# Cosine attention and a low-rank mixer with an MLP: a rebuild on 128-row token chunks, with the MLP cut into pieces placed by hand

## The chip, the cores and the metric

The kernel runs on one core of one Trainium2 chip. The metric is the device time of one execution in microseconds (us), the median of several. A core has TensorE (PE: matmuls, with its weight loads shown apart as PEld), VectorE (DVE), ScalarE (ACT), GpSimd (POOL) and SyncE (SP). PE writes its results into PSUM, which has eight banks; DVE and ACT carry them from there to SBUF. DMAs bring data from HBM to SBUF and back; here POOL and SP issue them. Each engine runs its own instructions in a fixed order and waits on semaphores for the others.

## The reference, cut to what matters

```python
# batch, heads, seq, head_dim = 8, 12, 448, 64;  rank 32;  d_model 768
q_n = q / (norm(q) + 1e-6);  k_n = k / (norm(k) + 1e-6)
scores = q_n @ k_n.T / tau                    # tau = 0.1
attn = exp(scores - max(scores));  attn /= sum(attn) + 1e-9
x = (attn @ v), heads side by side            # [8, 448, 768]
h = x.T @ U @ V                               # mixes the 448 tokens through rank 32
u = x + h.T
out = u + relu(u @ w_ch1) @ w_ch2             # 768 -> 3072 -> 768
```

Inputs and output are float32 in HBM. Both kernels compute in bfloat16 and accumulate in float32. Both leave the maximum out of the softmax, since a cosine over tau stays between -10 and 10.

## The kernel before, in words

The 448 tokens of a batch are held as 4 chunks of 112 rows (`SC = 4`, `SCH = 112`; token `4*s + c` is row s of chunk c). Heads go in pairs, 6 pairs a batch, 48 pairs in all.

`attention_pair` (L91 on) issues six DMAs from POOL's queue, which turn float32 into bfloat16 on the way (q L101, k L105, v L109). DVE squares and sums q and k (L118 to L121); ACT takes the logarithm (L124) and two exponentials (L125, L127), which give 1/norm; DVE scales q (L131). PE transposes q and k, 112 columns at a time (L138, L143). The two heads of a pair then lie in rows 0 to 63 and 64 to 127. DVE copies the transposed q out (L149) and writes the transposed k twice, once with the lower and once with the upper 64 rows zeroed by a mask (L151, L153), so that a score matmul over all 128 rows gives one head. There are 8 score matmuls a pair, 112 rows by 448 (L160), each followed by an exponential on ACT (L166), which carries 1/norm of k as its scale. The product with v is 32 matmuls a pair, 65 columns wide (L178); column 65 of v is one, so it gives the sum of the softmax. DVE divides (L185, L187) into `X_sb`.

`moe_stage0` transposes X (L199, L204), multiplies with U (L210, L216) and V (L221), and DVE adds h to the transposed X (L227). `moe_mlp1` (L235, L241) makes 24 chunks of 128 hidden units: 6 matmuls of 448 columns and one ReLU on ACT each. `moe_mlp2` (L248, L254) has the second weight matrix as the loaded operand and gives the transposed output, 6 chunks of 24 matmuls of 448 columns. `moe_store` transposes it back (L264, L270) and stores it from SP's queue (L271).

The MLP of a batch is emitted in 7 pieces between the pairs of the next batch (`emit_moe_piece`); a scheduler then orders each engine's instructions. The weights come in 30 DMAs from POOL's queue among the loads of batch 0 (L89). PSUM: two banks each for scores, av, transposes and everything of the mixer and the MLP.

## Time and profile before

| what | value |
|---|---|
| time, 3 runs | 819.03, 822.45 and 1068.92 us; median 822.45 |
| profiled execution: first to last instruction | 818.3 us |
| PE busy in it | 715.8 us (87%) |
| ACT busy | 494.6 us (60%), with 94 table loads in it |
| DVE busy | 307.0 us (38%) |
| POOL busy | 225.8 us (28%) |
| first MLP matmul of batch 0; of batch 7 | at 106.5 us; at 753.6 us |
| granted PE clock, mean | 0.991 |

The profiled execution lies 0.7 us under the fastest run and 4.1 us under the median, so what lies around the span is small; one of the three runs stands far off the two others. A row of the timeline gives start, length, engine, line, operation, written tile `<-` read tiles, shape, the number of instructions merged into it, and in brackets the idle time before it with what ended it. A row of the groups gives `busy us, mean ns of one`. Matmuls overlap in their pipeline, so the length of one is longer than its share of a stream: the rate is read from a merged row. In this program the stages are: batch 0's attention alone (to 106 us), seven stretches with the attention of one batch and the MLP of the one before, and the last MLP alone (from 753.6 us).

### The profile page before, as it was taken

The numbers are of one execution on the slowest core, as the hardware profiler recorded it, in microseconds if no ns is written. First come the engines' busy times: TensorE is split into PE (matmuls) and PEld (weight loads), VectorE is DVE, ScalarE is ACT, GpSimd is POOL, SyncE is SP. The second block draws the span as 40 slices with busy tenths as digits, with TensorE's granted clock in tenths as the row PEclk, the third lists the DMA queues.
The fourth block names the chain that finished last, engine by engine and source line by source line (L and its number), as shares of the span: only waits on it lengthen the run. The fifth ranks groups of instructions, "written<-read, shape, count | busy, mean of one in ns | idle before, by whom it ended". The sixth has DMA issues, their size and how long they took to land.

```text
span 818.3 us, 12706 instructions
## 1 busy us (share of the span) xinstructions
PE 715.8 (87%) x5104; PEld 426.3 (52%) x5104; DVE 307.0 (38%) x720; ACT 494.6 (60%) x862; POOL 225.8 (28%) x382
## 2 busy tenths in 40 slices
PE   2456777999989998899989998899989999999996
PEld 2244544555555555555545555455545556554553
DVE  2253673444434362344524362334523351223000
ACT  3457688954786379755777369755778357622411
POOL 6388832422423232322423231322232100000000
PEclk9999999999999999999999999999999999999999
DMA  8999942524434261524434261433442120002002
GB/s 122 181 149 149 79 29 18 36 18 85 31 22 30 18 96 12 35 19 85 28 24 29 18 97 12 27 25 75 34 29 18 12 68 1 2 1 68 1 0 68
DMA packets 142618, 37.84 MB, mean 46 GB/s; under 512 B 135104, under 2 KB 138208, under 8 KB 142560
## 3 DMA queue, kind: packets, MB, share of 16 engines
q0 software_dynamic: 138464, 26.03, 38.6%
q1 hardware_dynamic: 4096, 11.01, 4.2%
q8 instruction: 40, 0.66, 0.3%
q14 instruction: 18, 0.15, 0.1%
HBM read 52.02 MB, written 11.01 MB: 77 GB/s over the span
## 4 chain that ended last, share of the span: by engine, by line
PE 61%; ACT 16%; issue 8%; DMA 8%; POOL 4%; DVE 2%; DVEq 0%; POOLq 0%; ACTq 0%
PE m_ps L248 26%; PE m_ps L235 15%; PE sc_ps L160 8%; PE av_ps L178 6%; ACT L124 4%; ACT L166 3%; ACT attn_uT L166 3%; DMA v_pair<-in_v_dram 3%; DMA w_sb<-in_moe_w_ch_dram 3%; ACT relu L241 2%; DMA q_pair<-in_q_dram 2%; PE o_ps L264 1%; PE h_ps L221 1%; POOL v_pair L109 1%; ACT O_sb L270 1%
## 5 line engine op out<-in xcount | busy, mean ns | idle before, releaser
L166 ACT ACTIVATE attn_uT<-sc_ps,inv_qk 112x448 bf16<-112x448 f32 x384 | 221.1, 633 | 102.3 <-PE sc_ps L160 99.0
L235 PE MATMUL m_ps<-uT_all,w_sb 128*128 128x448 bf16 x1152 | 250.2, 356 | 10.3 <-ACT relu L241 9.7
L248 PE MATMUL m_ps<-relu,w_sb 128*128 128x448 bf16 x1152 | 234.6, 352 | 0.0
L160 PE MATMUL sc_ps<-qT,kTz 128*112 128x448 bf16 x384 | 141.0, 389 | 41.8 <-ACT attn_uT L166 25.0
L178 PEld LDWEIGHTS <-attn_uT 112*112 112x112 bf16 x1536 | 124.5, 141 | 81.2 <-issue 33.2
L235 PEld LDWEIGHTS <-w_sb 128*128 128x128 bf16 x1152 | 106.8, 99 | 105.8 <-issue 23.2
L248 PEld LDWEIGHTS <-w_sb 128*128 128x128 bf16 x1152 | 107.7, 98 | 91.6
L241 ACT ACTIVATE relu<-m_ps 128x448 bf16<-128x448 f32 x192 | 101.0, 539 | 89.2 <-PE m_ps L235 89.0
L178 PE MATMUL av_ps<-v_pair,attn_uT 112*112 112x65 bf16 x1536 | 145.2, 221 | 3.2 <-ACT attn_uT L166 3.2
L109 POOL DMA_DIRECT2D v_pair<-in_v_dram x96 | 66.9, 701 | 271.9 <-issue 263.0
L105 POOL DMA_DIRECT2D k_pair<-in_k_dram x96 | 66.8, 701 | 98.5 <-PE qkT_ps L143 84.0
L270 ACT CAST O_sb<-o_ps 112x768 f32<-112x768 bf16 x32 | 23.2, 808 | 100.4 <-PE o_ps L264 100.4
L254 DVE TENSOR_TENSOR uT_all<-m_ps,uT_all 128x448 bf16<-128x448 f32 x48 | 29.9, 622 | 120.2 <-PE m_ps L248 120.2
L160 PEld LDWEIGHTS <-kTz 128*112 128x112 bf16 x384 | 52.2, 142 | 42.3 <-DVE kTz L151 24.9
L101 POOL DMA_DIRECT2D q_pair<-in_q_dram x96 | 67.1, 704 | 9.1 <-DVE qn_pair L131 3.6
L118 DVE TENSOR_TENSOR sq_tmp<-q_pair 112x512 bf16<-112x512 bf16 x48 | 20.3, 422 | 111.6 <-DMA q_pair<-in_q_dram 111.6
L185 DVE RECIPROCAL rd<-av_ps 112x4 f32<-112x4 f32 x96 | 17.2, 180 | 118.2 <-PE av_ps L178 117.9
L124 ACT ACT_TABLE_LOAD x47 | 60.3, 1283 | 1.9 <-PEq L334 0.7
L138 PE MATMUL qkT_ps<-ident,qn_pair 112*128 112x112 bf16 x192 | 27.6, 225 | 38.0 <-DVE qn_pair L131 34.4
L131 DVE TENSOR_TENSOR qn_pair<-q_pair,inv_qk 112x512 bf16<-112x512 bf16 x48 | 33.1, 689 | 43.8 <-ACT inv_qk L125 43.8
L166 ACT ACT_TABLE_LOAD x37 | 47.5, 1283 | 0.7
L187 DVE TENSOR_TENSOR X_sb<-av_ps,rd 112x256 bf16<-112x256 f32 x96 | 40.6, 423 | 2.6
(42 smaller groups left out, 457.4 us busy)
## 6 DMA issues: line engine op xcount, KB each, us to landing
out_dram<-O_sb SPq DMA_DIRECT2D x32, 336.0 KB, 3.6
q_pair<-in_q_dram POOLq DMA_DIRECT2D x96, 56.0 KB, 2.8
k_pair<-in_k_dram POOLq DMA_DIRECT2D x96, 56.0 KB, 2.8
v_pair<-in_v_dram POOLq DMA_DIRECT2D x96, 56.0 KB, 2.8
w_sb<-in_moe_w_ch_dram POOLq DMA_DIRECT2D x6, 768.0 KB, 9.2
w_sb<-in_moe_w_ch_dram POOLq DMA_DIRECT2D x24, 192.0 KB, 5.7
U_sb<-in_moe_U_dram POOLq DMA_DIRECT2D x1, 28.0 KB, 2.5
V_sb<-in_moe_V_dram POOLq DMA_DIRECT2D x1, 28.0 KB, 2.0
```

The source lines that it names most:

```text
L101: nc.gpsimd.dma_start(out=q_pair[:, :, hh, :], in_=q[b, h0 + hh].rearrange("(s c) d -> s c d", c=SC))
L105: nc.gpsimd.dma_start(out=k_pair[:, :, hh, :], in_=k[b, h0 + hh].rearrange("(s c) d -> s c d", c=SC))
L109: nc.gpsimd.dma_start(out=v_pair[:, :, hh, 0:D], in_=v[b, h0 + hh].rearrange("(s c) d -> s c d", c=SC))
L124: nc.scalar.activation(lnq2, q2k2, AF.Ln)
L131: nc.vector.tensor_mul(qn_pair, q_pair, inv_qk[:, :, :, 0:1].to_broadcast([SCH, SC, 2, D]))
L160: nc.tensor.matmul(out=sc_ps, lhsT=kTz[:, hh, jc, :], rhs=qT.rearrange("p a b -> p (a b)"), start=True, stop=True,)
L166: nc.scalar.activation(out=attn_uT[:, hh, jc, :], in_=sc_ps, func=AF.Exp, scale=inv_qk[:, jc, hh, 1:2],)
L178: nc.tensor.matmul(out=av_ps[:, ic, 0:D + 1], lhsT=attn_uT[:, hh, jc, ic * SCH:(ic + 1) * SCH], rhs=v_pair[:, jc, hh, :], start=(jc == 0), ...
L187: nc.vector.tensor_mul(X_sb[:, :, c0:c0 + D], av_ps[:, :, 0:D], rd.to_broadcast([SCH, SC, D]))
L235: nc.tensor.matmul(out=m1_ps, lhsT=w1_sb[:, cc, nch * 128:(nch + 1) * 128], rhs=uT_all[:, cc, :], start=(cc == 0), stop=(cc == CC - 1),)
L241: nc.scalar.activation(out=relu1[:, nch, :], in_=m1_ps, func=AF.Relu)
L248: nc.tensor.matmul(out=m2_ps, lhsT=w2_sb[:, nch, cc * 128:(cc + 1) * 128], rhs=relu1[:, nch, :], start=(nch == 0), stop=(nch == NC - 1),)
```

## The change

Nearly all of the kernel is written anew; the mathematics is the same, with 1e-6 added to the norms as in the reference.

- **Chunks.** The first 256 tokens of a batch lie 4 to a row in rows 0 to 63, the other 192 lie 3 to a row in rows 64 to 127. That makes three chunks of 128 tokens and a last one of 64. For k and v the second head of a pair is laid out the other way round (192 tokens in rows 0 to 63, 256 in rows 64 to 127), so that the two half chunks of a pair share one chunk of 128 rows.
- **Loads.** q, k and v come as float32 through SP's queue, 10 DMAs for a group of two pairs (one pair in the first two groups), into two sets of staging tiles. DVE squares, sums and scales from float32; POOL turns k and v into bfloat16.
- **ACT.** One table set with both logarithm and exponential is loaded at the start. Half of the ReLUs and half of the output copies go to DVE.
- **Scores.** 7 matmuls a pair: 6 over 64 rows (head 0 in rows 0 to 63, head 1 in rows 64 to 127, without masks) and one over 128 rows for the shared chunk. Four PSUM banks.
- **Product with v.** 28 matmuls a pair with 128 loaded columns, in two halves (`step_V`), one PSUM bank.
- **Mixer.** `step_MH` sums the mixing and X itself (through the identity matrix) in one bank; DVE copies it once. `step_T`, `step_MA` and `step_MH` share one bank.
- **Second MLP matmul.** The hidden units are now the loaded operand (128 tokens), the weights stream with 384 columns; the output comes in token rows, with u added through the identity, and the transposes back are gone. Two batches share `relu`, so that a pair of batches has 7 chunks of 128 tokens: 3 after an even batch, 4 after an odd one.
- **Order.** PE's and POOL's instructions stand as written. The MLP is a list of steps, 24 of `steps_m1` and 24 or 32 of `steps_m2`, of 6 matmuls each (the last of a half has 3 more), and the loop deals them out between the attention steps.

```diff
+    nc.scalar.preload_act_table_set("natural_log_exp_and_others")
+    order = ctx.enter_context(tc.manual_schedule(engines={PE, POOL}))
...
+    def load_group(gi):
...
+        nc.sync.dma_start(out=dst(qst[s], L, slice(0, nh), 4), in_=src(q, allh, 0, 256, 4))
+        nc.sync.dma_start(out=dst(qst[s], U2, slice(0, nh), 3), in_=src(q, allh, 256, 448, 3))
+        for x, t in ((k, kst[s]), (v, vst[s])):
...
+    def prep_group(gi):
...
+        for j, t in ((0, qst[s]), (1, kst[s])):
+            sq = work.tile([128, NG * 4, D], FP, name="sq", tag="sq", bufs=2)
+            nc.vector.tensor_mul(sq[:, 0:nh * 4, :], flat(t), flat(t))
+            nc.vector.reduce_sum(ss[:, j, 0:nh * 4], sq[:, 0:nh * 4, :], axis=AX.X)
...
+        for j in range(n):
+            nc.gpsimd.tensor_copy(out=kb[:, j, :, :, :],
+                                  in_=kst[s][:, 2 * j:2 * j + 2, :, :].rearrange("p h c d -> p c h d"))
...
+        nc.gpsimd.tensor_copy(out=flat(vv)[:, :, 0:D], in_=flat(vst[s]))
+        nc.scalar.activation(ss[:, :, 0:nh * 4], ss[:, :, 0:nh * 4], AF.Ln)
+        nc.scalar.activation(ss[:, :, 0:nh * 4], ss[:, :, 0:nh * 4], AF.Exp, scale=0.5)
...
+    def step_T(b, p):
...
+        tp = psum.tile([128, 8, 128], BF, name="tp", tag="ps_x", bufs=1)
...
+        nc.vector.tensor_copy(out=t.rearrange("p a b -> p (a b)"),
+                              in_=tp.rearrange("p a b -> p (a b)"))
...
+    def scores(b, p, slots):
...
+        for s in slots:
+            sc = psum.tile([128, S], FP, name="sc", tag="ps_sc", bufs=4)
+            if s == 6:
+                nc.tensor.matmul(out=sc, lhsT=t[:, 1, 384:512], rhs=t[:, 0, 0:S],
+                                 start=True, stop=True)
+                col = (2 * j) * 4 + 3
+            else:
+                h, c = divmod(s, 3)
+                r = slice(64 * h, 64 * h + 64)
+                nc.tensor.matmul(out=sc, lhsT=t[r, 1, c * 128:(c + 1) * 128], rhs=t[r, 0, 0:S],
+                                 start=True, stop=True)
+                col = (2 * j + h) * 4 + c
+            nc.scalar.activation(out=e[:, s, 0:S], in_=sc, func=AF.Exp, scale=inv[:, 1, col:col + 1])
...
+    def step_V(b, p, half):
...
+        av = psum.tile([128, 2, 2, D + 1], FP, name="av", tag="ps_av", bufs=1)
...
+    def step_MA(b, half):
...
+        ap = psum.tile([128, HC], FP, name="ap", tag="ps_x", bufs=1)
...
+    def step_MH(b, cc):
+        up = psum.tile([128, S], FP, name="up", tag="ps_x", bufs=1)
+        nc.tensor.matmul(out=up, lhsT=A_of[b][:, cc * 128:(cc + 1) * 128], rhs=V_sb,
+                         start=True, stop=False, skip_group_check=True)
+        for c in range(4):
+            n = 128 if c < 3 else 64
+            nc.tensor.matmul(out=up[:, c * 128:c * 128 + n],
+                             lhsT=X[:, c, cc * 128:(cc + 1) * 128], rhs=ident[:, 0:n],
+                             start=False, stop=(c == 3), skip_group_check=True)
+        nc.vector.tensor_copy(out=u_of(b)[:, cc, 0:S], in_=up)
...
+            mp = psum.tile([128, S], FP, name="mp", tag="ps_m", bufs=2)
...
+            if f % 2 == 0:
+                nc.scalar.activation(out=relu[:, f, o:o + S], in_=mp, func=AF.Relu)
+            else:
+                nc.vector.tensor_scalar_max(out=relu[:, f, o:o + S], in0=mp, scalar1=0.0)
...
+                state[ci] = work.tile([128, C], FP, name="o_sb", tag="o_sb", bufs=3)
...
+            for f in range(lo, hi):
+                nc.tensor.matmul(out=mp, lhsT=relu[:, f, r0:r0 + 128],
+                                 rhs=w2_sb[:, f, half * HC:(half + 1) * HC],
+                                 start=(f == 0), stop=False, skip_group_check=True)
...
+        if n < len(pairs):
+            parts.append((lambda: scores(b, p, (6, 0, 3, 1)), 2))
+            parts.append((lambda: scores(b, p, (4, 2, 5)), 2))
+        if n > 0:
+            pb, pp = pairs[n - 1]
+            parts.append((lambda: step_V(pb, pp, 0), 1))
+            parts.append((lambda: step_V(pb, pp, 1), 1))
+        if n + 1 < len(pairs):
+            tb, tp_ = pairs[n + 1]
+            parts.append((lambda: step_T(tb, tp_), 1))
+        if first and n > 0:
+            pb = b - 1
+            for half in range(2):
+                parts.append((lambda half=half: step_MA(pb, half), 1))
+            for cc in range(CC):
+                parts.append((lambda cc=cc: step_MH(pb, cc), 1))
...
+        for fn, w in parts:
+            fn()
+            acc += w
+            want = nf * acc // weight
+            f(want - given)
+            given = want
```

A pair's iteration gets 7 to 10 MLP steps; 10 are kept for the first pair of the next batch, where the mixer stands.

**ACT in the attention of one batch beside the MLP of the one before** (`lnq` and `inv_qk` are the norms, `attn_uT` the exponentials, `relu` the MLP's first half). Before:

```order
L125 ACTIVATE inv_qk<-lnq_2896,b_lt 112x8
L127 ACTIVATE inv_qk<-lnq_2896,b_zero 112x8
L124 ACT_TABLE_LOAD
L124 ACTIVATE lnq_3416<-q2k_3410 112x16
L241 ACTIVATE relu_1979<-m_ps 128x448 x3
L166 ACT_TABLE_LOAD
L166 ACTIVATE attn_uT<-sc_ps,inv_qk 112x448 x8
```

ACT in the same place of the changed kernel (`ss` are the norms, `E` the exponentials):

```order
L232 ACTIVATE E_105<-sc,inv 128x448 x4
L300 ACTIVATE relu<-mp 128x448
L232 ACTIVATE E_105<-sc,inv 128x448 x3
L185 ACTIVATE ss<-ss 128x32
L300 ACTIVATE relu<-mp 128x448
L186 ACTIVATE ss<-ss 128x32
L300 ACTIVATE relu<-mp 128x448 x2
```

The table loads are gone, and with the ReLUs of odd chunks on DVE a pair has 7 exponentials instead of 8 and half the ReLUs.

**DVE where one batch's attention ends and its mixer is worked** (`XT_all`, `uT_all`: transposed X and u; `rd`, `X_sb`: the division after the product with v). Before:

```order
L204 COPY XT_all<-xt_ps 128x448
L227 TENSOR_TENSOR uT_all<-h_ps,XT_all 128x448
L204 COPY XT_all<-xt_ps 128x448 x2
L227 TENSOR_TENSOR uT_all<-h_ps,XT_all 128x448
L204 COPY XT_all<-xt_ps 128x448 x2
L227 TENSOR_TENSOR uT_all<-h_ps,XT_all 128x448
L185 RECIPROCAL rd<-av_ps 112x4
L120 TENSOR_TENSOR sq_tmp<-k_pair 112x512
L187 TENSOR_TENSOR X_sb<-av_ps,rd 112x4x64
```

DVE in the same place of the changed kernel (`uE` is u of an even batch, `sq` the squares of a later group):

```order
L285 CAST uE<-up 128x448 x2
L176 TENSOR_TENSOR sq<-qst_72 128x1024
L285 CAST uE<-up 128x448
L177 TENSOR_REDUCE ss<-sq 128x16
L285 CAST uE<-up 128x448
L176 TENSOR_TENSOR sq<-kst_73 128x1024
L285 CAST uE<-up 128x448
L177 TENSOR_REDUCE ss<-sq 128x16
L285 CAST uE<-up 128x448
```

One copy a step is left of the two operations, and four operations on 1024 float32 elements a row stand between these copies.

**SP's queue in the second half of an MLP.** Before, it held stores alone:

```order
L271 DMA out_dram<-O_sb 112x768 [waits DMAHW0_49,Activation_49]
L271 DMA out_dram<-O_sb 112x768 [waits DMAHW1_49,Activation_49]
L271 DMA out_dram<-O_sb 112x768 [waits DMAHW2_49,Activation_49]
L271 DMA out_dram<-O_sb 112x768 [waits DMAHW3_49,Activation_49]
L271 DMA out_dram<-O_sb 112x768 [waits DMAHW4_49,Activation_49]
```

SP in the changed kernel (`qst`, `kst`, `vst` are the staging tiles, `o_sb` the output rows):

```order
L151 DMA qst_72<-in_q_dram 64x4x256 [waits DMAHW4_49,DVE_49]
L152 DMA qst_72<-in_q_dram 64x4x192 [waits DMAHW5_49]
L155 DMA kst_76<-in_k_dram 64x2x256 [waits DMAHW6_49,Pool_49]
L156 DMA kst_76<-in_k_dram 64x2x192 [waits DMAHW7_49]
L347 DMA out_dram<-o_sb 64x768 [waits DMAHW0_49,DVE_49,Activation_49]
L350 DMA out_dram<-o_sb 64x768 [waits DMAHW1_49]
L157 DMA kst_76<-in_k_dram 64x2x192 [waits DMAHW2_49]
L158 DMA kst_76<-in_k_dram 64x2x256 [waits DMAHW3_49]
```

Stores stand behind loads that wait for DVE or POOL to have read a staging tile.

More of the change, by code (lines that the diff above doesn't have):

```diff
@@ L13 @@
 ALU = mybir.AluOpType
+AX = mybir.AxisListType
+PE = mybir.EngineType.PE
+POOL = mybir.EngineType.Pool
 @with_exitstack
@@ L305 @@
[L305 to L317 removed]
+    uE = const.tile([128, CC, S], BF, name="uE")
@@ new lines, with u_of @@
+    A_of = {}
+    def step_MA(b, half):
+        if half == 0:
+            A_of[b] = work.tile([128, C], BF, name="A_sb", tag="A_sb", bufs=1)
+        ap = psum.tile([128, HC], FP, name="ap", tag="ps_x", bufs=1)
+        for c in range(4):
+            nc.tensor.matmul(out=ap, lhsT=U_sb[:, c, :], rhs=X[:, c, half * HC:(half + 1) * HC],
+                             start=(c == 0), stop=(c == 3))
+        nc.scalar.copy(out=A_of[b][:, half * HC:(half + 1) * HC], in_=ap)
+    def u_of(b):
+        return uE if b % 2 == 0 else uO
@@ L321 @@
+    f(len(fill))
 _INS = ['q', 'k', 'v', 'tau', 'moe_U', 'moe_V', 'moe_w_ch1', 'moe_w_ch2']
```

484 lines of the change are left out of this document (245 added, 239 removed).

## The prediction

> **What bounds the kernel now.** I read the page first, then PE's timeline at the stage borders and in full streams, the groups of ACT, PEld and DVE, and the chain of waits of the start. The page's busy times and its chain:
>
> ```profile
> span 818.3 us, 12706 instructions
> PE 715.8 (87%) x5104; PEld 426.3 (52%) x5104; DVE 307.0 (38%) x720; ACT 494.6 (60%) x862; POOL 225.8 (28%) x382
> PE 61%; ACT 16%; issue 8%; DMA 8%; POOL 4%; DVE 2%; DVEq 0%; POOLq 0%; ACTq 0%
> ```
>
> PE is the bound, but 87% is an average over stages. PE's timeline, at the first MLP matmul of batch 0, at the first of batch 7, and in the second half of that last MLP:
>
> ```profile
> 106.48 5.83 PE L235 MATMUL m_ps<-uT_all,w_sb 128*128 128x448 bf16 x30 [0.31 <-DVE uT_all L227]
> ...
> 753.58 28.74 PE L235 MATMUL m_ps<-uT_all,w_sb 128*128 128x448 bf16 x144 [0.18 <-DVE uT_all L227]
> 782.15 27.40 PE L248 MATMUL m_ps<-relu,w_sb 128*128 128x448 bf16 x144
> ```
>
> So there are a head of 106.5 us, seven periods of (753.58 - 106.48) / 7 = 92.4 us, and a tail of 818.3 - 753.6 = 64.7 us. The last row gives the rate of a 448-column matmul in a stream: 27.40 / 144 = 0.190 us. The other rates, from the same timeline:
>
> ```profile
> 745.05 0.33 PE L210 MATMUL a_ps<-X_sb,U_sb 112*128 112x384 bf16 x1
> 745.53 0.98 PE L210 MATMUL a_ps<-X_sb,U_sb 112*128 112x384 bf16 x5
> 746.52 0.49 PE L264 MATMUL o_ps<-ident,uT_all 128*112 128x128 bf16 x6
> 809.39 0.72 PE L264 MATMUL o_ps<-ident,uT_all 128*112 128x128 bf16 x10
> 309.21 0.19 PE L178 MATMUL av_ps<-v_pair,attn_uT 112*112 112x65 bf16 x1
> 312.30 0.86 PE L178 MATMUL av_ps<-v_pair,attn_uT 112*112 112x65 bf16 x13
> 329.50 0.21 PE L143 MATMUL qkT_ps<-ident,k_pair 112*128 112x112 bf16 x1
> 329.55 0.21 PE L138 MATMUL qkT_ps<-ident,qn_pair 112*128 112x112 bf16 x1
> 307.95 0.35 PE L160 MATMUL sc_ps<-qT,kTz 128*112 128x448 bf16 x1 [1.44 <-ACT attn_uT L166]
> ```
>
> 384 columns: (0.98 - 0.33) / 4 = 0.1625 us. 128 columns: (0.72 - 0.49) / 4 = 0.0575. The 65-column product with v: (0.86 - 0.19) / 12 = 0.056. Transposes of 112 columns start 0.050 apart. A 448-column matmul alone lasts 0.35, so the pipeline's tail is 0.35 - 0.19 = 0.16.
>
> By these rates PE's streams before sum to 2304 x 0.190 (MLP) + 384 x 0.190 (scores) + 1536 x 0.056 (av) + 576 x 0.050 and 192 x 0.0575 (transposes) + 64 x 0.1625 and 48 x 0.190 (mixer) = 656 us, or 82.0 a batch. A period takes 92.4, so 10.4 us of each is lost. The last row above shows one such loss: PE waits 1.44 us for an exponential. ACT's timeline and groups show what it stood behind:
>
> ```profile
> 305.98 1.28 ACT L166 ACT_TABLE_LOAD   x1
> ...
> L124 ACT ACT_TABLE_LOAD x47 | 60.3, 1283 | 1.9 <-PEq L334 0.7 <-DVE q2k L121 0.3
> L166 ACT ACT_TABLE_LOAD x37 | 47.5, 1283 | 0.7
> L125 ACT ACT_TABLE_LOAD x10 | 12.8, 1283 | 0.2
> L166 ACT ACTIVATE attn_uT<-sc_ps,inv_qk 112x448 bf16<-112x448 f32 x384 | 221.1, 633 | 102.3 <-PE sc_ps L160 99.0
> L241 ACT ACTIVATE relu<-m_ps 128x448 bf16<-128x448 f32 x192 | 101.0, 539 | 89.2 <-PE m_ps L235 89.0
> ```
>
> 94 table loads, 120.6 us. The head has another bound. Its chain of waits:
>
> ```profile
> 10.98 8.14 DMA w_sb<-in_moe_w_ch_dram
> ...
> 19.41 9.53 DMA v_pair<-in_v_dram
> ```
>
> The first pairs wait for loads that queue with the weights.
>
> **The change part by part: PE's streams.**
> - First MLP matmul: 1152 x 0.190 = 218.9, as before. Second: 1344 x 0.1625 = 218.4; 384 columns instead of 448 but more matmuls, so nothing is won there.
> - Identity matmuls, 168 for the residual and 192 in the mixer, at the 128-column rate: 360 x 0.0575 = 20.7. Other mixer matmuls: 48 x 0.190 + 64 x 0.1625 = 19.5. Transposes of q and k: 384 x 0.0575 = 22.1. The transposes of X and of the output are gone.
> - Product with v: 192 of 130 columns, 11.0, and 1152 of 65 columns. The trace has no 65-column matmul with 128 loaded columns. Above: today's 0.056. Below: 65 columns at 0.190 / 448 a column, 0.028. The weight loads speak for less than today:
>
> ```profile
> L178 PEld LDWEIGHTS <-attn_uT 112*112 112x112 bf16 x1536 | 124.5, 141 | 81.2 <-issue 33.2 <-ACT attn_uT L166 18.9 <-PE m_ps L248 5.0
> L248 PEld LDWEIGHTS <-w_sb 128*128 128x128 bf16 x1152 | 107.7, 98 | 91.6
> ```
>
>   128 columns load in 98 ns, 112 in 141. The transposes, with 128-column loads, run at 0.050 with 112 columns to stream, so the load costs at most that. I take 0.040: 57 us in all (43 to 75).
> - Scores: no half-height matmul is in the trace. In the order 6, 0, 3, 1 and 4, 2, 5, if 0 runs beside 3 and 4 beside 2, a pair takes 5 lengths, 0.95 us. If none do, 7 lengths, 1.33; and if PE drains at each of the four changes between full and half height, 4 x 0.16 more, 1.97. I take 1.3, near the middle: 62 us (46 to 95).
>
> Sum 619 us, 77.4 a batch (73.6 to 83.7), against 82.0.
>
> **Other engines.** ACT: 336 exponentials at 221.1 / 384 = 0.576, 96 ReLUs at 0.526 and some 60 us at most for copies and norms make about 300 us. DVE's rows:
>
> ```profile
> L119 DVE TENSOR_REDUCE q2k<-sq_tmp 112x8 f32<-112x512 bf16 x48 | 32.8, 684 | 3.3
> L131 DVE TENSOR_TENSOR qn_pair<-q_pair,inv_qk 112x512 bf16<-112x512 bf16 x48 | 33.1, 689 | 43.8 <-ACT inv_qk L125 43.8
> L187 DVE TENSOR_TENSOR X_sb<-av_ps,rd 112x256 bf16<-112x256 f32 x96 | 40.6, 423 | 2.6
> L185 DVE RECIPROCAL rd<-av_ps 112x4 f32<-112x4 f32 x96 | 17.2, 180 | 118.2 <-PE av_ps L178 117.9
> L227 DVE TENSOR_TENSOR uT_all<-h_ps,XT_all 128x448 bf16<-128x448 f32 x48 | 29.2, 615 | 0.7
> L149 DVE COPY qT<-qkT_ps 128x448 bf16<-128x448 bf16 x48 | 18.5, 386 | 48.3 <-PE qkT_ps L143 48.0
> ```
>
> From 256 to 512 elements costs 0.27 us, so 1024 take about 0.69 + 2 x 0.27 = 1.2. Some 95 squares and sums of that size (115 us), 48 scalings (33), 96 divisions (58), 48 transposed copies (34), 48 copies of u (30), 96 ReLUs (60), 28 output copies (15) and small ones (20) make 365 us. Both stay at about half of the span; neither becomes the bound, so what they cost is delay.
>
> **Delays on PE.** The added waits are for banks. `step_T`, `step_MA` and `step_MH` share one. Behind a T, `step_MA` follows at once: it waits for the copy of 1024 elements, 0.7 us (0.88 if it scaled with L149) and the 0.16 tail. Two of the six `step_MH` follow another with no MLP step between: 0.62 + 0.16 + a signal, 0.85 each. Together 2.6 us a batch; PE's whole queue stands behind them. Between the halves of `step_V`, 0.18 + 0.42 + 0.16 us hide under one MLP step (6 x 0.1625 = 0.98 or 6 x 0.190 = 1.14) unless DVE is in one of its long operations. These fill 12 x 1.2 + 6 x 0.69 = 18.5 us of a period, 22%; a pass that meets one waits 0.6 on average, and with 12 v halves, 6 transposes and 8 mixer steps that is 26 x 0.22 x 0.6 = 3.4 us. With 0.5 for ReLUs held behind exponentials: 6.5 us a batch (3 to 11; before, 10.4). Period: 83.9 (77 to 94).
>
> **Head.** The page's rows of the queues and of SP's stores:
>
> ```profile
> q0 software_dynamic: 138464, 26.03, 38.6%
> q1 hardware_dynamic: 4096, 11.01, 4.2%
> ...
> out_dram<-O_sb SPq DMA_DIRECT2D x32, 336.0 KB, 3.6
> ```
>
> A store of 336 KB lands in 3.6 us; I take 5 for the first loads. The norms take 4 x 0.69 + 0.69 and about 1.5 of small ones, the transposes and their copy 1.5: the first exponential comes near 12. A pair needs 7 x 0.576 = 4.0 us of exponentials and some 0.3 of norms, six pairs 26: to 38; 5 us more for loads beside the weights. The hardware queue moved 11.01 MB in 4.2% of 818.3 us on all 16 engines, 320 GB/s: batch 0's 4.1 MB is 13 us of it, all weights 59 us if they go no faster, so the second matrix is there when wanted, near 93 us. After the last pair the mixer of batch 0 runs with no MLP step to cover it, 8 steps of about 1.3 us and the last v: 14 us. Head 57 us (46 to 68).
>
> **Tail.** 144 x 0.190 and 4 chunks of 48 x 0.1625 + 6 x 0.0575 make 60.0; times (28.74 + 27.40) / (288 x 0.190) = 1.026 it is 61.5, and 5 us for the last copy and store: 66.5.
>
> Seven periods hold four of the lighter even MLPs: -4. Sum: 57 + 7 x 83.9 - 4 + 66.5 = 707 us of span. The span before lies 0.7 to 4.1 us below its times; with 2 us, **709 us**, 0.86 of the median.
>
> **Rivals.**
> - *Everything is covered*: tiles run side by side, v at 0.028, 3 us of delay, a head of 48. 48 + 7 x 76.6 - 4 + 66 = 646 us. For it: PE in the last MLP loses 2.6% only. Against: the single banks. Chance 0.22.
> - *The tiles pay a drain and gain nothing*: 1.97 us a pair, 4 us more a batch: 709 + 28 = 737 us. The row that bears on it is the 0.16 tail of a lone matmul. Chance 0.12. [...]
> - *DVE's long operations stand in front of the banks' passes* with their full length: 18.5 + 2.6 instead of 6.5 us a batch, 7 x 14.6 more: 811 us, no change. The order shows squares and sums between the copies of u. Chance 0.06. [...]
> - *Stores behind loads on SP*: a load waits up to a group's time, 84 / 3 = 28 us, for its staging tile, and the stores behind it hold the three `o_sb`. Two chunks (11 us each with a pair's attention) pass before PE needs the third; with a store's 3.6 us 28 - 22 + 3.6 = 9.6 us are lost a group: 709 + 21 x 9.6 = 911 us, slower. From 6.2 us a group on it is slower by 2%. Against: stores stand after two loads, not after a whole group's. Chance 0.05.
>
> **Numbers.** My forecast has 0.55. The range 655 to 765 holds it, the drains and most of the covered case. About 2% is what a measurement tells from no change: below 806 or above 839. The forecast, the covered case, the drains and part of the DVE case are faster: 0.92; the rest of DVE's and a mild form of SP's are the same: 0.04; SP's full form: 0.04.
>
> **What would show it.** One table load on ACT; first MLP matmul near 57 us; periods near 84; L297 and L323 at 0.19 and 0.1625 a matmul; L248 near 0.04; idle time of PE before `ap` and `up` ended by DVE and ACT, under 7 us a batch. I am wrong if the head passes 70 us, if the score rows L223 and L229 take over 2 us a pair, or if PE waits in L323 for SP.

## The result and the profile after

The changed kernel takes 752.8 us (median of 5 executions), the kernel before 819.0 (of 5 too; three of them are in the table above): a ratio of 0.919, 95% interval 0.916 to 0.922. The forecast was 709 with a range of 655 to 765, so direction and range held and the size did not: 44 us of the expected gain are missing.

In what follows `step_T`, `step_V`, `step_MA` and `step_MH` are L207/L209, L241/L248, L269 and L278/L282 of the changed kernel; L297 and L323 are the two MLP matmuls, L176/L177 the squares and their sums, L256 the division, L211 the copy of the transposes. The page of its profiled execution (757.1 us, the longest of the five by 4 us):

```profile
span 755.4 us, 12104 instructions
...
PE 650.7 (86%) x5032; PEld 366.3 (48%) x5032; DVE 350.5 (46%) x674; ACT 263.6 (35%) x527; POOL 77.8 (10%) x106
...
PE 61%; DMA 15%; DVE 13%; SPq 5%; issue 3%; ACT 1%; POOL 1%; POOLq 0%; DVEq 0%
PE mp L297 24%; PE mp L323 21%; DMA qst<-in_q_dram 9%; DVE sq L176 5%; PE sc L229 5%; PE av L248 4%; DMA vst<-in_v_dram 3%; DVE ss L177 2%; DMA kst<-in_k_dram 2%; PE av L241 1%; SPq L151 1%; PE ap L269 1%; PE tp L207 1%; PE sc L223 1%; SPq L158 1%
```

PE is about as full as before (87%) and ACT fell from 60% to 35%, but the chain now has 28% of DMA and DVE, where it had 10%. PE's timeline, at the two stage borders that the prediction used:

```profile
107.17 4.07 PE L297 MATMUL mp<-uE,w_sb 128*128 128x448 bf16 x12
...
690.86 27.40 PE L297 MATMUL mp<-uO,w_sb 128*128 128x448 bf16 x144
```

| stage | before | forecast | after |
|---|---|---|---|
| head, to the first MLP matmul | 106.5 | 57 | 107.2 |
| one period, of seven | 92.4 | 83.3 (83.9, less 4 / 7) | 83.4 |
| tail | 64.7 | 66.5 | 64.5 |
| span | 818.3 | 707 | 755.4 |

The whole gain of 62.9 us is 7 x 9.0 us in the periods, as forecast. The head, which was to give 49 us, gave nothing. PE's timeline there shows four long waits, three between the halves of a `step_V` and one for the copy of the transposes:

```profile
41.59 0.86 PE L248 MATMUL av<-v,E 128*128 128x65 bf16 x12
51.27 0.40 PE L241 MATMUL av<-v,E 128*128 128x130 bf16 x2 [8.82 <-DVE X L256]
...
68.08 0.40 PE L241 MATMUL av<-v,E 128*128 128x130 bf16 x2 [10.26 <-DVE X L256]
...
79.41 0.40 PE L241 MATMUL av<-v,E 128*128 128x130 bf16 x2 [4.79 <-DVE X L256]
...
85.47 0.55 PE L223 MATMUL sc<-qkT 128*128 128x448 bf16 x1 [4.16 <-DVE qkT L211]
```

A division takes 0.42 us; it is late because of what stands in front of it. DVE's timeline in the first of these waits:

```profile
42.60 1.23 DVE L176 TENSOR_TENSOR sq<-qst 128x1024 f32<-128x1024 f32 x1 [4.04 <-DMA qst<-in_q_dram]
...
48.40 1.23 DVE L176 TENSOR_TENSOR sq<-kst 128x1024 f32<-128x1024 f32 x1 [3.32 <-DMA kst<-in_k_dram]
49.54 0.18 DVE L255 RECIPROCAL rd<-av 128x4 f32<-128x4 f32 x1
...
50.80 0.42 DVE L256 TENSOR_TENSOR X<-av,rd 128x256 bf16<-128x256 f32 x1
```

These squares belong to batch 1's first group. The scheduler put them ahead of a division of batch 0, as if their loads were there; the loads run beside the weights' (233 GB/s from 30 to 60 us, the DMA engines at 90% or more in the page's slices there) and have not landed: the two squares wait 4.04 and 3.32 us for them. DVE waits in order, the only `av` bank stays taken, and PE's queue waits with it, 8.82 us.

### The profile page after: what moved, and what is told of

Same layout as the page of the kernel before. It is cut to its first block, busy times and chain, and to the rows that moved or that the text cites. A ratio compares the mean times of both kernels' runs of the same rounds, so it can differ in the third digit from the quotient of the medians.

```text
span 755.4 us, 12104 instructions
## 1 busy us (share of the span) xinstructions
PE 650.7 (86%) x5032; PEld 366.3 (48%) x5032; DVE 350.5 (46%) x674; ACT 263.6 (35%) x527; POOL 77.8 (10%) x106
## 4 chain that ended last, share of the span: by engine, by line
PE 61%; DMA 15%; DVE 13%; SPq 5%; issue 3%; ACT 1%; POOL 1%; POOLq 0%; DVEq 0%
PE mp L297 24%; PE mp L323 21%; DMA qst<-in_q_dram 9%; DVE sq L176 5%; PE sc L229 5%; PE av L248 4%; DMA vst<-in_v_dram 3%; DVE ss L177 2%; DMA kst<-in_k_dram 2%; PE av L241 1%; SPq L151 1%; PE ap L269 1%; PE tp L207 1%; PE sc L223 1%; SPq L158 1%
## 5 line engine op out<-in xcount | busy, mean ns | idle before, releaser
L323 PE MATMUL mp<-w_sb,relu 128*128 128x384 bf16 x1344 | 248.1, 330 | 0.0
L232 ACT ACTIVATE E<-sc,inv 128x448 bf16<-128x448 f32 x336 | 185.4, 637 | 147.4 <-PE sc L223 133.7
L323 PEld LDWEIGHTS <-relu 128*128 128x128 bf16 x1344 | 123.4, 99 | 84.5 <-issue 16.7
L297 PEld LDWEIGHTS <-w_sb 128*128 128x128 bf16 x1152 | 106.0, 98 | 107.8 <-issue 22.2
L297 PE MATMUL mp<-uE,w_sb 128*128 128x448 bf16 x576 | 121.3, 356 | 0.0
L297 PE MATMUL mp<-uO,w_sb 128*128 128x448 bf16 x576 | 115.6, 353 | 2.5 <-DVE relu L302 2.5
L302 DVE TENSOR_SCALAR relu<-mp 128x448 bf16<-128x448 f32 x96 | 59.7, 621 | 105.2 <-PE mp L297 105.2
L241 PE MATMUL av<-v,E 128*128 128x130 bf16 x192 | 28.4, 231 | 43.5 <-DVE X L256 43.5
L229 PE MATMUL sc<-qkT 64*128 64x448 bf16 x288 | 62.4, 386 | 0.0
L177 DVE TENSOR_REDUCE ss<-sq 128x16 f32<-128x1024 f32 (+1 forms) x50 | 58.1, 1161 | 0.3
L248 PE MATMUL av<-v,E 128*128 128x65 bf16 x1152 | 56.2, 201 | 0.0
L248 PEld LDWEIGHTS <-E 128*128 128x128 bf16 x1152 | 49.6, 102 | 0.0
L241 PEld LDWEIGHTS <-E 128*128 128x128 bf16 x192 | 16.5, 99 | 64.6 <-DVE X L256 49.0
L176 DVE TENSOR_TENSOR sq<-qst 128x1024 f32<-128x1024 f32 (+1 forms) x25 | 29.5, 1178 | 38.4 <-DMA qst<-in_q_dram 38.3
L256 DVE TENSOR_TENSOR X<-av,rd 128x256 bf16<-128x256 f32 x96 | 40.4, 421 | 2.2
L211 DVE COPY qkT<-tp 128x1024 bf16<-128x1024 bf16 x48 | 32.8, 684 | 15.5 <-PE tp L209 15.5
```

The source lines that it names most:

```text
L176: nc.vector.tensor_mul(sq[:, 0:nh * 4, :], flat(t), flat(t))
L177: nc.vector.reduce_sum(ss[:, j, 0:nh * 4], sq[:, 0:nh * 4, :], axis=AX.X)
L229: nc.tensor.matmul(out=sc, lhsT=t[r, 1, c * 128:(c + 1) * 128], rhs=t[r, 0, 0:S], start=True, stop=True)
L232: nc.scalar.activation(out=e[:, s, 0:S], in_=sc, func=AF.Exp, scale=inv[:, 1, col:col + 1])
L241: nc.tensor.matmul(out=av[:, i, :, :], lhsT=e[:, 6, ic * 128:(ic + 1) * 128], rhs=vv[:, 2 * j:2 * j + 2, 3, :], start=(i == 0), stop=False ...
L248: nc.tensor.matmul(out=av[:, i, h, :], lhsT=e[:, 3 * h + c, ic * 128:(ic + 1) * 128], rhs=vv[:, 2 * j + h, c, :], start=False, stop=(i == ...
```

## The experiments

**The head: loads, weights or order.** Four kernels, one execution each, read by their first MLP matmul.

*The weights later* (their place on POOL's queue, behind the casts of batch 0's last group):

```diff
-                for _ in range(2 if prepped[0] < 5 else 3):
+                for _ in range({2: 1, 4: 4, 5: 2, 6: 2}.get(prepped[0], 0)):
```

> Only the place of the eight weight loads on POOL's queue is changed: behind the casts of batch 0's last group (near 33 us, where the profile of the changed kernel has them from 23 to 58 us). Theory A, DVE's order: VectorE has the squares of batch 1's groups, which wait for their loads, in front of the divisions that free the one av bank of batch 0. Batch 1's first group now lands before the weights' traffic, at 36 to 40 us, and its squares no longer hold a division; the second and third still land beside the weights and hold one or two. First MLP matmul at 75 to 95 us (107.2 before), total 722 to 742 us. Theory B, bandwidth: what counts is when the DMA engines are through with 20 MB at 233 GB/s, 86 to 93 us, in whatever order: first MLP matmul 100 to 108, total 745 to 755. Theory C, cover: with the weights out of batch 0's way nothing else holds PE, as the prediction took it: 57 us, total 703.

Measured: first MLP matmul at 105.5 us, total 754.8. Batch 1's first group held nothing, but the waits came back later: 9.23 us (at 60.4) and 4.80 (71.7) for a division, 3.90 (77.5) for the copy of the transposes, 5.27 (95.0) for a copy of u, each behind squares of batch 1's second and third group and of batch 2's first, which now landed beside the weights. The number is the one that theory B gave.

*Few weights* (23 in 24 of the weights are not loaded, so the output is another one; only the time is read):

```diff
-    for i in range(4):
-        weight_loads.append(lambda i=i: load_w1(i * 768, (i + 1) * 768))
-    for i in range(4):
-        weight_loads.append(lambda i=i: load_w2(i * 6, (i + 1) * 6))
+    weight_loads.append(lambda: load_w1(0, 128))
+    weight_loads.append(lambda: load_w2(0, 1))
...
-                nc.tensor.matmul(out=mp, lhsT=w1_sb[:, cc, f * 128:(f + 1) * 128],
+                nc.tensor.matmul(out=mp, lhsT=w1_sb[:, cc, 0:128],
...
-                                 rhs=w2_sb[:, f, half * HC:(half + 1) * HC],
+                                 rhs=w2_sb[:, 0, half * HC:(half + 1) * HC],
```

> One sixth of the first weight matrix's first load and one of 24 row blocks of the second are loaded, and every MLP step reads these same 128 columns and 128 rows: the weights' traffic is left out (9.4 MB of SBUF writes), the instructions on PE, VectorE and ScalarE are the same. This is the head with batch 0's and batch 1's loads alone. Theories A and C: all loads land ahead of their squares, no division is held: first MLP matmul 50 to 60 us, total 697 to 712. Theory B: 10.7 MB at 233 GB/s, 46 us, so no other bound than PE's own chain: the same 50 to 60. A fourth possibility, SP's issue of one load each 0.64 us: 70 issues to batch 1's second group make 45 us, then 60 to 70.

Measured: 84.3 us, total 727.8. The long waits are gone, 23 us of the head with them, but no theory had 84. PE's timeline of this kernel, one pair of the head (its L221/L227 are the scores, L239/L246 the product with v, L205/L207 the transposes):

```profile
55.70 0.56 PE L221 MATMUL sc<-qkT 128*128 128x448 bf16 x1 [0.79 <-DVE qkT L209]
56.18 2.37 PE L227 MATMUL sc<-qkT 64*128 64x448 bf16 x6
58.48 0.40 PE L239 MATMUL av<-v,E 128*128 128x130 bf16 x2
58.67 0.87 PE L246 MATMUL av<-v,E 128*128 128x65 bf16 x12
60.28 0.40 PE L239 MATMUL av<-v,E 128*128 128x130 bf16 x2 [0.74 <-DVE X L254]
60.48 0.86 PE L246 MATMUL av<-v,E 128*128 128x65 bf16 x12
61.15 0.62 PE L205 MATMUL tp<-ident,qn 128*128 128x128 bf16 x4
61.56 0.63 PE L207 MATMUL tp<-ident,kb 128*128 128x128 bf16 x4
62.98 0.55 PE L221 MATMUL sc<-qkT 128*128 128x448 bf16 x1 [0.79 <-DVE qkT L209]
```

The pair takes 62.98 - 55.70 = 7.3 us, with no load in it. PE goes through scores, two halves of v and transposes one after the other, with two waits of 0.74 and 0.79 us that nothing covers. And the matmuls run at half rate: from start to start a half of v takes 0.87 us and four transposes 0.41, where beside the MLP they take 0.50 and 0.22. The scores take 2.8 us, since the last three of the seven wait for a bank at the pace of the exponentials: the seven of a pair take 3.78 us on ACT, 0.54 each.

*Order alone, in blocks* (DVE's order by hand; norms of batch 1's first two groups behind the attention steps):

```diff
-    order = ctx.enter_context(tc.manual_schedule(engines={PE, POOL}))
+    order = ctx.enter_context(tc.manual_schedule(engines={PE, POOL, DVE}))
...
-        if n < len(pairs):
+        if n in (NP - 2, NP):
+            load_ahead(n + 2)
+        elif n < len(pairs):
             advance(n + 2)
...
+        if n in (NP - 2, NP):
+            advance(n + 2)
```

> VectorE's order is written by hand (as the program text stands), and the norms of batch 1's first two groups are put behind the divisions of the attention steps beside which they stood; loads, weights and their queues stay as they are. Theory A: the three waits for a division of 8.8, 10.3 and 4.8 us at 51, 68 and 79 us go; what is left is the wait for batch 1's first group before its transpose: first MLP matmul 78 to 88 us. Theory B: first MLP matmul 100 to 108 us, since the loads land no earlier. The periods behind it will be longer than 83.4 us, because a group's norms now stand in one block of some 8 us on VectorE: total not compared.

Measured: 93.4 us, between the two theories' ranges (total 775.7). The four waits are gone with the weights loading as early as ever, so they were the order's. The hand order made three of its own, 9.21, 4.43 and 4.65 us, where a whole group's norms stand in front of a copy or a division that PE wants; without them the head would be some 75 (93.4 less their 18.3, an estimate).

*Both*:

> The weights behind batch 0's loads and the norms of batch 1's first two groups behind the divisions, both. Theory A: neither weights nor order hold batch 0: first MLP matmul 60 to 72 us. Theory B: 93 us or more. Theory C: as with the weights moved alone, 57.

Measured: 93.6 us (total 775.8), 0.2 from the kernel without the weights moved. Theory A's 60 to 72 failed for the same three waits. The number is in theory B's range, but not for its reason: loads that land earlier changed nothing, and from 20 us to the last v DVE never waits for a load in either of the two. A kernel without such waits had to decide between them; it comes below.

**The pairs of the head.** On the kernel with few weights (one execution), the next pair's transposes between the halves of `step_V`:

```diff
+        if not fill and n > 0 and n + 1 < len(pairs):
+            parts[-2:] = [parts[-1], parts[-2]] if not first else parts[-2:]
```

> On the kernel with the weights' traffic left out (first MLP matmul at 84.31 us, a pair each 7.3 to 8.3 us): where no MLP step is at hand, the transposes of the next pair stand between the two halves of step_V and no longer behind both. Theory A, PE's order: a pair of the head costs the sum of its steps on PE at the low clock (scores 2.8, two halves of v 0.9 each, transposes 1.0) and the two waits of 0.74 and 0.79 us that stand alone between them; each wait now lies beside a step: about 1.5 us less in each of five pairs, first MLP matmul at 75 to 79 us. Theory B: a pair costs what ScalarE and the loads need, and the order changes nothing: 83 to 85 us.

Measured: 81.7 us (84.3 without it). From the third pair's scores on, four pairs took 6.9, 7.5, 6.5 and 6.7 us, 27.5 together, against 8.5, 8.3, 8.3 and 7.3, 32.3: 1.2 less a pair. Of this 1.7 went again after the last pair, in a wait of 1.96 us for a division and in the mixer, which ran at half rate throughout, where the kernel without the change has two steps at the full rate (from 74.26 to 76.1 us). Theory A's direction; a pair gave 1.2 of its 1.5 us, the head 2.6 of some 7.5, and 81.7 lies outside its range.

**The scores.** Three kernels change only which rows or which order the score matmuls have. The first leaves out the separation of the two heads, so its output is another one.

```diff
-                r = slice(64 * h, 64 * h + 64)
+                r = slice(0, 128)
```

> The six half-height score matmuls of a pair take all 128 rows (which adds the two heads' scores, so part of the result is another one): no tiles, no change between full and half height, the same 48 x 7 matmuls. Theory A: tiles run side by side and the changes cost; the profile has the two parts of a pair at 0.77 + 0.55 = 1.32 us from start to next start, five lengths of 0.19 are 0.95, so the changes cost 0.37 and eat what the tiles gain: seven lengths, 1.33 us a pair, and the time stays within 5 us of 752.8. Theory B: no cost at the changes (1.32 has another reason): 0.38 us a pair more, 42 pairs beside the MLP, 16 us slower. Theory C: the tiles gain nothing and the changes cost 0.6: 25 us faster.

```diff
-            parts.append((lambda: scores(b, p, (6, 0, 3, 1)), 2))
-            parts.append((lambda: scores(b, p, (4, 2, 5)), 2))
+            parts.append((lambda: scores(b, p, (6, 0, 1, 2)), 2))
+            parts.append((lambda: scores(b, p, (3, 4, 5)), 2))
```

> The slots of a pair are taken as 6, 0, 1, 2 and 3, 4, 5 in place of 6, 0, 3, 1 and 4, 2, 5: neighbours of half height are always in the same half, so none can run side by side, and the number of changes between full and half height is as before. Theory A (side by side, and changes cost 0.37 a pair): 7 lengths + 0.37 = 1.70 us a pair, 42 x 0.38 = 16 us slower than 752.8, near 769. Theory C (tiles gain nothing): no change, within 4 us.

```diff
+            parts.append((lambda: scores(b, p, (6, 0, 3)), 2))
+            parts.append((lambda: scores(b, p, (1, 4, 2, 5)), 2))
```

> The slots of a pair are taken as 6, 0, 3 and 1, 4, 2, 5: three twos of opposite halves, so four lengths in place of five. Theory A: 0.19 us a pair less, 42 pairs: 8 us faster, near 745, if the wait for ScalarE's exponentials does not take it back (the second part now brings four scores). Theory C: within 4 us of 752.8.

Measured: 752.2 us at full height (ratio to before 0.918, 0.915 to 0.920), 760.5 with neighbours in one half (0.928, 0.924 to 0.932), 747.1 with all paired (0.911, 0.909 to 0.914), beside 752.8 (0.919). The changed kernel was timed at another time than these three; by its ratio it would take 754.5 beside them, so differences of some 2 us are not told apart. PE's timeline at a pair of the changed kernel, and then of the one at full height:

```profile
621.05 0.35 PE L223 MATMUL sc<-qkT 128*128 128x448 bf16 x1
621.34 0.55 PE L229 MATMUL sc<-qkT 64*128 64x448 bf16 x3
621.82 2.44 PE L297 MATMUL mp<-uE,w_sb 128*128 128x448 bf16 x12
624.20 0.55 PE L229 MATMUL sc<-qkT 64*128 64x448 bf16 x3
```

```profile
616.64 0.35 PE L223 MATMUL sc<-qkT 128*128 128x448 bf16 x1
616.83 0.73 PE L229 MATMUL sc<-qkT 128*128 128x448 bf16 x3
617.40 2.43 PE L297 MATMUL mp<-uE,w_sb 128*128 128x448 bf16 x12
619.67 0.73 PE L229 MATMUL sc<-qkT 128*128 128x448 bf16 x3
```

At full height the second matmul starts 0.19 us after the first; with tiles 0.29. Three take 0.57 to the next start at full height, 0.48 with tiles: two lengths and again 0.10. Twelve MLP matmuls up to the next scores take 2.27 and 2.38. With all three in one half the same row of the timeline is 0.74 long instead of 0.55; with all paired, two take 0.36 and four 0.55. So tiles of opposite halves do run side by side here, and each change between full and half height costs 0.10 us. Five lengths and four changes are 1.35 us a pair, seven lengths 1.33: the tiles gained nothing, and theory A holds. The 0.10 us is less than the 0.16 of a lone matmul's tail, which the prediction's upper end has at each change. With all paired a length is saved; 42 x 0.19 = 8.0 were expected and 5.7 came. With none side by side 16 were expected and 7.7 came: PE's waits for DVE from 190 to 685 us fell from 33.9 to 29.1 us, 2.0 of it before divisions and 2.3 before ReLUs; that is more than half of the difference, and the rest is not shown. Theory A had this time as PE's alone.

**Order, then banks.** A group's norms cut in seven pieces, one behind each attention step, in DVE's order by hand. Nothing else is changed; the weights' loads keep their place behind POOL's casts. `due` holds the pieces, `g()` emits the next one, and `g(9)` all that are left, ahead of transposes that need them:

```diff
+        pieces = [lambda: square(0, qst[s]), lambda: total(0),
+                  lambda: (square(1, kst[s]), casts()), lambda: (total(1), roots()),
+                  lambda: None, lambda: (inverse(), scale(0))]
...
-            prep_group(prepped[0])
+            due.extend(prep_group(prepped[0]))
...
-        for fn, w in parts:
+        for i, (fn, w) in enumerate(parts):
+            if need and i == at_T:
+                g(9)
             fn()
+            if n > 0 or i == len(parts) - 1:
+                g()
```

> One of the five edits alone: VectorE's order by hand, with a group's norms in pieces behind the attention steps. Slots, weights, transposes and banks are those of the changed kernel. Theory A (the order holds the head and lengthens the periods): the head is that of the five edits, 75, and five gaps of 1.4 us more for the transposes behind both halves of step_V: first MLP matmul 80 to 86 us though the weights load as early as before; periods 78.5 + 0.8 for the unpaired slots = 79.3 us; total 83 + 7 x 79.3 + 64.5 + 2 = 705 us (698 to 715). Theory B (the weights' place did it, the order little): first MLP matmul over 95 us, periods 82 to 83, total over 735.

Measured: 705.6 us (0.861, 0.859 to 0.864), the expected 705. PE's timeline at its two borders, and then the waits of PE for divisions over the whole span (us in total, times, the longest), of the changed kernel and of this one:

```profile
85.54 4.55 PE L320 MATMUL mp<-uE,w_sb 128*128 128x448 bf16 x12
...
639.95 27.40 PE L320 MATMUL mp<-uO,w_sb 128*128 128x448 bf16 x144
```

```profile
PE av L241 <- DVE X L256: 43.5, 17, 10.3
```

```profile
PE av L264 <- DVE X L279: 4.4, 6, 0.7
```

First MLP matmul 85.5, (639.95 - 85.54) / 7 = 79.2 a period. POOL issues the weights' loads from 23.6 to 57.1 us, in the changed kernel from 23.1 to 57.8, and the head is within 1.2 us of the one with few weights: theory B is out.

Two banks for transposes and mixer, three for scores, which then come in three parts, on the kernel with all slots paired (747.1):

```diff
-            sc = psum.tile([128, S], FP, name="sc", tag="ps_sc", bufs=4)
+            sc = psum.tile([128, S], FP, name="sc", tag="ps_sc", bufs=3)
-        up = psum.tile([128, S], FP, name="up", tag="ps_x", bufs=1)
+        up = psum.tile([128, S], FP, name="up", tag="ps_x", bufs=2)
...
-            parts.append((lambda: scores(b, p, (1, 4, 2, 5)), 2))
+            parts.append((lambda: scores(b, p, (1, 4)), 1))
+            parts.append((lambda: scores(b, p, (2, 5)), 1))
```

> The kernel with the slots 6, 0, 3 and 1, 4, 2, 5 (747.1 us), with two banks for the transposes and the mixer, three for the scores, and the scores in three parts, 6, 0, 3 and 1, 4 and 2, 5; VectorE's order is the scheduler's. Theory A (the bank's waits and VectorE's order are two separate losses): the gain is that of the banks under the hand order, 22 us less: 725 us (720 to 731). Theory B (under the scheduler's order VectorE's long operations stand in front of the banks' passes, and a second bank only moves the wait to the next division): gain under 10 us, 737 or more.

Measured: 719.9 us (0.879, 0.877 to 0.882), 27 us less; the head stayed (105.0), the period fell from 82.2 to 78.3. Theory A, and somewhat more than it gave (720 to 731). The banks and the three parts were not tried apart.

All together, first with one bank (pieces, slots, weights later, transposes between the halves), then with two and the scores in three parts:

> Five edits together: the slots as 6, 0, 3 and 1, 4, 2, 5; VectorE's order by hand; a group's norms cut into seven pieces, one behind each attention step, so that no square of batch 1 stands in front of a division of batch 0; the weights behind batch 0's loads; the next pair's transposes between the halves of step_V where no MLP step is at hand. Theory A (the head is lost to VectorE's order and to PE's serial pairs): the head of 81.7 us that the kernel with few weights and the moved transposes had, less the waits for divisions left in it (1.3, 0.9, 1.0, 1.1 and 2.0 us): first MLP matmul 74 to 80 us; with the 5.7 us of the paired slots the time is 752.8 - 29 - 6 = 718 us (708 to 728). Theory B (the loads set the head once the weights are in): first MLP matmul over 90 us, 735 or more. Against both: the hand order is worse than the scheduler's beside the MLP, then the periods grow past 82.2 us.

> As the kernel before it in this series, but with two banks for the transposes and the mixer and three for the scores, which then come in three parts, 6, 0, 3 and 1, 4 and 2, 5. Theory A (the shared bank costs what the prediction's term says, 2.6 us a batch, and five waits of 0.7 to 0.8 us in the head): 7 x 2.6 + 4 = 22 us less, and two more changes of height at 0.1 a pair, 42 x 0.2 = 8 us more: 14 us faster than that kernel. Theory B: PE then waits for the third score bank, as an exponential takes 0.58 us and a score 0.19: no gain, or a loss up to 10 us.

Measured: 691.6 us (0.842, 0.839 to 0.844) and 668.8 (0.814, 0.812 to 0.815). First MLP matmul at 75.0 and 70.2, periods 78.5 and 76.0. The head is where theory A had it; the first total is 26 us under the 718 expected, because I had left out what the order does for the periods (79.2 instead of 83.4 in the kernel with the order alone). The second bank, with the third score part, gave 22.8 us where 14 were expected. In parts of these two heads PE runs at the full rate (a half of v in 0.54 us at 58.69 and at 59.50), which it never does in the changed kernel's; what that gave is not told apart from the edits. The last kernel's page, three of its waits, and its timeline at the borders:

```profile
span 667.0 us, 12095 instructions
...
PE 632.4 (95%) x5032; PEld 360.5 (54%) x5032; DVE 367.6 (55%) x674; ACT 269.6 (40%) x527; POOL 71.9 (11%) x106
```

```profile
PE tp L230 <- DVE qn L210: 16.7, 3, 10.4
PE sc L252 <- ACT E L255: 3.8, 16, 0.4
PE av L264 <- DVE X L279: 3.8, 8, 0.6
```

```profile
70.21 2.44 PE L320 MATMUL mp<-uE,w_sb 128*128 128x448 bf16 x12
...
602.45 27.40 PE L320 MATMUL mp<-uO,w_sb 128*128 128x448 bf16 x144
```

This kernel beats both: by the two ratios to before it takes 0.8135 / 0.9192 = 0.885 of the changed one's time. PE's long waits that are left are the three for the first norms, before 30 us. What moving the weights gave within these two was not tried alone.

## Why the prediction was right and wrong

**Head: wrong, by 50.2 us, which is the whole miss** (the periods differ by 0.4 and the tail by 2.0 the other way: 48.4 of span; the profiled execution is 4 us above the median). Its own range was 46 to 68. The range of the total reached up for drains and for waits in the periods, so that it holds 752.8 is luck. Three steps of the prediction failed, and one held.
- *"A pair needs 7 x 0.576 = 4.0 us of exponentials and some 0.3 of norms, six pairs 26: to 38."* I took ACT for the bound of a stage in which PE alternates, in order, with DVE's copies and divisions. In the kernel with the order alone the six pairs take from 12.18 to 62.86, 50.7 us; the shortest takes 7.3, and the others more by what their norms need. That is 24.7 us. I also used the rates of the MLP stretches in a stage whose matmuls run at half of them.
- *"5 us more for loads beside the weights."* I saw that loads queue with the weights and asked when a pair's own loads land; those of batch 0 were in time. What I did not ask was who stands behind an instruction that waits for a load. 107.2 - 85.5 = 21.6 us went to DVE's order, 16.6 more than the term.
- *"14 us"* for the mixer of batch 0 and the last v. From the first `step_MA` at 92.75 to the first MLP matmul are 14.4. But the seventh pair's scores, the last v and the transposes of the eighth pair stand between the sixth pair and it: 22.7 us in the kernel with the order alone, 8.7 more.
- *"the first exponential comes near 12"*: the first scores start at 12.7.

24.7 + 16.6 + 8.7 = 50.0.

**Periods: right, from two terms that were each off a little.** PE's streams were put at 77.4 us a batch. The last kernel has a period of 76.0 with 0.5 of waits in it, so they come to some 75.5. The 65-column product is 0.03, not 0.040 (12 in 0.54 us), so a pair's v takes 0.98 us between starts and a batch's 5.9, not 7.1. The scores' 1.3 us was right for another reason than the one given: it was a middle between ends, and is five lengths and four changes. Delays were put at 6.5 and are 83.4 - 75.5 = 7.9; that the two errors nearly cancel is luck. PE's waits in the six periods from 190 to 691 us (us in total, times, the longest):

```profile
PE av L241 <- DVE X L256: 13.4, 9, 2.4
PE ap L269 <- DVE qkT L211: 7.1, 5, 1.5
PE up L278 <- DVE uE L285: 6.8, 8, 1.2
PE up L278 <- DVE uO L285: 3.7, 4, 1.1
PE mp L297 <- DVE relu L302: 2.5, 3, 1.3
PE sc L223 <- DVE qkT L211: 0.4, 2, 0.2
```

A batch: 1.2 before `ap` (0.9 forecast), 1.75 before `up` (1.7), 2.2 for divisions (3.4 for all passes), 0.4 for ReLUs (0.5): 5.65 in all. Of the other 2.2 some 1.1 is PE's clock (last section); the rest stays open. DVE's order alone took 4.2 of the 7.9 (83.4 to 79.2): PE's waits in six periods fell from 33.9 to 18.2 us (there from 164.7 to 640 us), 2.6 a batch, and the granted clock stayed at 1.00.

**Tail: right**, 64.5 for 66.5.

**The signs.** One table load, as said, and both MLP matmuls keep their rates. PE's idle time before `ap` and `up` is 2.9 us a batch, under 7, and DVE ends it. L248 takes 0.03, not 0.04. The head passed 70, which I had named as the mark of a wrong forecast; the score rows stayed under 2 us; PE never waited in L323 for SP.

**Rivals.** *Everything is covered* (646): not this kernel, but its period of 76.6, less 4 / 7, is the last kernel's 76.0. The floor was right, its parts were not: 73.6 of streams and 3 of waits, where the last kernel has some 75.5 and 0.5. *Tiles pay a drain and gain nothing* (737): true of the balance, 1.35 against 1.33, and not of its price, since both halves of it were mis-sized: tiles do run side by side (three scores in 0.55 us, 0.74 in one half), and no run shows the 0.16 us of drain that it has at each change: a change was measured at 0.10, which makes 1.35 us a pair where it had 1.97. *DVE's long operations in front* (811): the mechanism that cost most, in another place. I priced it at DVE's own durations beside the MLP; it cost 4.2 us a batch there (2.2 of them waits for divisions) and 21.6 in the head, where the operation in front waits itself. *Stores behind loads on SP*: no trace of it.

## What to carry to other kernels

DVE, which runs in order, passed late loads on to what stood behind the squares that waited for them, and that cost 21.6 us of this head: go through an engine's order at the places where loads are slow, and put what waits for a DMA behind what frees a bank, or cut it in pieces between them. The head, a stage without filler work, wasn't bounded by ACT's sum (3.78 us of exponentials a pair) but by the in-order path through the engines (7.3 us a pair in the kernel with few weights), at the rate that matmuls had in this stage (0.87 us for a half of v, 0.50 beside the MLP): add up that path for such a stage. Row tiles gained nothing with two twos and four changes a pair (1.35 us for 1.33) and 5.7 us in all with three twos: count whether enough twos stand together to pay for the changes around them.

## What the runs showed of the hardware

**In the changed kernel's periods PE's granted clock read 0.50 four times for 3.41 us, each time behind 3.41 us with 1.96 to 2.36 us of idle time in them.** PE's timeline of the changed kernel after a division that came late:

```profile
335.60 0.29 PE L241 MATMUL av<-v,E 128*128 128x130 bf16 x2 [2.27 <-DVE X L256]
335.73 0.80 PE L248 MATMUL av<-v,E 128*128 128x65 bf16 x12
336.34 2.11 PE L323 MATMUL mp<-w_sb,relu 128*128 128x384 bf16 x6
338.25 0.53 PE L330 MATMUL mp<-ident,uE 128*128 128x128 bf16 x3
...
345.32 1.14 PE L323 MATMUL mp<-w_sb,relu 128*128 128x384 bf16 x6
346.30 0.28 PE L241 MATMUL av<-v,E 128*128 128x130 bf16 x2
```

Six matmuls take 1.91 us to the next start, and 9 us later 0.98. From 110 to 691 us the granted clock reads 0.50 in four stretches of 3.41 us, from 226.55, 335.78, 448.42 and 509.86 us on, and 1.00 in the rest. Their starts lie 109.23, 112.64 and 61.44 us apart, which is 32, 33 and 18 times 3.413 us. With the time cut into steps of that length from these starts, PE is idle for 1.96, 2.27, 2.01 and 2.36 us in the step before each. No other step between 110 and 691 us has more than 1.82 (the one from 308.47). How long a single wait is does not tell the four apart: a wait of 1.36 us at 226.39 was followed by a fall, one of 1.95 at 163.18, which lies across two steps, was not. That the idle time of a whole step counts is my reading of these four falls; no run tests it. It isn't all, since in the kernel before the clock read 0.50 for 3.41 us from 752.92 us on, behind a step with 0.71 us of idle time. The stretch shown costs 0.93 us in these six matmuls and 0.7 in the smaller steps around them, so 1.6 beyond its wait; four like it are 6.4 us, 1.1 a batch in six periods.

In the changed kernel's head v and transposes run at the half rate from first to last (12 products of 65 columns in 0.86 us, 0.54 beside the MLP), and so do the first MLP matmuls behind it (12 in 4.07 us, 2.44 later). The granted clock reads 1.00 from 0 to 107 us, so the durations must be read. What lets the rate rise stays open: in the kernel with few weights and moved transposes the profile has PE busy for the whole 6.5 us from 44.69 us on, and a half of v still takes 0.86 at 50.40, while in the last kernel's head, which has waits, single halves run at the full rate (0.54 for a half of v at 59.50, and again 0.87 at 61.40). So in these runs 1.96 us of idle time in a step stood ahead of a fall, and 6.5 us of busy time brought no rise.

**A change between full and half height cost 0.10 us at each edge here**, also at the edge to the MLP's matmuls (2.38 for 2.27 us above).

**Two of POOL's casts took 1.06 us longer beside one of DVE's squares.** POOL's timeline of the changed kernel, two casts without and two with a square beside them (DVE's square at 48.40, above):

```profile
23.98 1.17 POOL L181 CAST kb<-kst 128x512 bf16<-128x512 f32 x2
...
48.43 2.23 POOL L181 CAST kb<-kst 128x512 bf16<-128x512 f32 x2 [8.32 <-DMA kst<-in_k_dram]
```

The casts take 1.06 us longer, nearly the square's 1.23, and this square no longer than others (1.22 at 19.31). In the head four such pairs of casts stand beside a square, at 31.40, 48.43, 65.29 and 83.21 us, and take 2.14 to 2.23; the two without, at 23.98 and 92.25, take 1.17 each. In the kernel with the order alone the square of the same k stands behind a division whose matmuls start at 49.08 us, so it does not run beside these casts, and the weights load as here:

```profile
47.95 1.17 POOL L187 CAST kb<-kst 128x512 bf16<-128x512 f32 x2 [8.59 <-DMA kst<-in_k_dram]
```

So the longer time goes with the square and not with the loads: at 23.98, too, the DMAs move 213 GB/s, and 229 at 48.43. What holds the casts beside a square, these runs do not show. No wait of PE ends with POOL, which is busy 10% of the span.
